# Batch 0 of a fused attention and FFN kernel: v scaled on GpSimd, numerators scaled and divided in PSUM, and all engines' work in a new order

## The chip, the core and the metric

One core of a Trainium2 chip. The time is that of one execution on the device, in microseconds (us), the median of several. The core's engines run at their own pace and wait for each other by semaphores: TensorE (PE, with its weight loads PEld), VectorE (DVE), ScalarE (ACT), GpSimd (POOL) and SyncE (SP, which here only issues DMAs). POOL and ACT issue DMAs too.

## The reference

Linear attention with a Hedgehog feature map, then a gated FFN. Batch 8, 8 heads, 576 positions, head size 64, 128 features; FFN 512 to 1536 to 512 over all 4608 tokens.

```python
def phi(x):
    proj = np.einsum('bhsd,df->bhsf', x, w_phi)
    proj = proj - np.max(np.abs(proj), axis=-1, keepdims=True)
    return np.concatenate([np.exp(proj), np.exp(-proj)], axis=-1)
q_p, k_p = (phi(q), phi(k))
kv = np.einsum('bhsf,bhsd->bhfd', k_p, v)
z = np.sum(k_p, axis=2)
num = np.einsum('bhsf,bhfd->bhsd', q_p, kv)
den = np.einsum('bhsf,bhf->bhs', q_p, z)[..., None] + 1e-06
attn = num / den                      # then heads side by side: x, 4608 x 512
out = (np.maximum(x @ w_gate, 0.0) * (x @ w_val)) @ w_out
```

## The kernel before

The order of all work is a table, ORDER, of some 2340 words; a loop reads it from left to right and calls for each word the function do_xx, which records one step. So the table fixes the order on every engine, DMA issues included; there is no other scheduler. `ke.0.1.2.0:0@kp0` means step ke with arguments batch 0, head group 1, token quarter 2, sign 0, in PSUM bank 0, with its output in buffer 0 of the ring kp. There are 8 PSUM banks, named by hand.

A batch goes through these steps (the first argument is the batch):

- Loads: lk, lm (k), lq, ln (q), wl (wv and wg in thirds of 512 columns) and wo on POOL's queue, with v of batch 0 (lv.0); lv and lw of the other batches on SP's.
- phi of k: the transposed k (kT) times w_phi on PE (k3 in batch 0, kr later), exponentials with both signs on ACT (ke, L688, into kp), the largest absolute value on DVE (kx, L696, into mk), and its exponentials on ACT (kk, L705, into ek). The heads stand in three groups: 0 to 1, 2 to 4, 5 to 7.
- v times ek: vs on POOL (L745, and vo L757 for the column of ones), vq on POOL for the last 64 positions (L773, into vr). In batch 0 before, head group 0 and vr were scaled on DVE instead (vd L726, vz L678), from an ek that ACT had put into PSUM (kp L716).
- kv on PE (L794), from kp, vs and vr, copied to SBUF by ACT (kc) or DVE (kd), both L805.
- phi of q: qb or qc on PE, qe on ACT (L869, into qp), qx on DVE (L877, the maximum), then qy, qz, qu and qw (ACT, L910, into cq: the factor between the two signs).
- numerators, per chunk of 128 tokens: before, all batches had nu on PE (L917, both signs side by side, in three head groups), nt on DVE (L938: the second sign times cq, into t), nv on DVE (L948: first sign plus t, into u), nr on DVE (L956, reciprocal of the denominator) and nx on POOL (L960, division, into xu).
- xu is transposed: in batch 0 by PE (xp) and a copy (xa on ACT L1011, xc on DVE L1005), later by DMA (xt).
- FFN of batch 0: in quarters of tokens and groups of four 128-column blocks, pv and pg on PE (L1224: 16 matmuls each, with wv and wg), pa (ACT L1239), pb (DVE L1245: relu times val, into h), fo (L1256). Batches 1 to 8 (8 are the left-over tokens of all batches): fv and fg (L1097), va on ACT or vb on DVE (the copy of val), ga (DVE L1118). Batches 7 and 8 are multiplied by a scheme of seven products for eight (fi, L1194), and so is the second FFN product (fw, L1361), with sums made on POOL (ps, xs, wt).
- zz multiplies zeros on PE (L455), in otherwise idle time ahead of the first FFN product.

Of the kernel before, what the change touches and what calls it, by code (L numbers as in the profile page):

```python
# [17 lines left out]
wd kh.0:1@kT0 sl k3.1.0:45 ke.0.1.0.0:4@kp0 w1:6 kg.1:2 kx.0.1.1:5@mk0 kx.0.1.0:4 wa:6 zz.2:7  # L18
k3.1.1:01 ke.0.1.3.0:1 lm.0.1 kx.0.1.2:0 zz.3:3 k0.2:2 lq.0.1 ke.0.1.3.1:1 k1.2:2@kT1 ke.0.1.0.1:4
zz.3:7 k0.0:6 ke.0.1.2.1:0 ke.0.1.1.1:5 k3.2.1:37 ke.0.1.2.0:0 kx.0.1.3:1 ms.2 lw.0.0 lw.0.1  # L20
k1.0:6@kT2 zz.5:4 k3.0.1:21 kk.0.1.0@ek0 k3.0.0:04 ke.0.1.1.0:5 ke.0.0.3.0:1@kp1 q0.1:5 lq.0.0
kx.0.2.3:7@mk1 kx.0.2.2:3 kk.0.1.1 ke.0.2.2.0:3@kp2 kx.0.0.0:0@mk2 kx.0.0.2:2 lv.0.1 ke.0.2.2.1:3
ke.0.0.1.1:4 kx.0.0.3:1 q1.1:5@qT0 ke.0.0.1.0:4 ke.0.0.3.1:1 lv.0.0 zz.6:6 q0.0:6 kx.0.0.1:4 wl.0.1
zz.4:3 k3.2.0:31 lv.0.2 ke.0.2.3.0:7 ke.0.0.2.1:2 ke.0.0.0.1:0 q1.0:6@qT1 ke.0.2.3.1:7 kx.0.2.1:1
zz.1:5 qb.1.1:5 zz.3:4 qb.0.1:4 kx.0.2.0:3 ke.0.0.0.0:0 zz.2:7 qb.0.0:0 qx.0.0.1:4 ke.0.0.2.0:2
zz.1:6 qb.1.0:2 qx.0.1.1:5 zz.7:7 qy.0.1:6 kp.0.0.0:0 ke.0.2.0.0:3 lk.1.3 kk.0.2.1@ek1 kp.0.0.1:0
kk.0.2.0 ke.0.2.1.1:1 vo.1@vs0 qx.0.1.0:2 qe.0.0.1.0:4@qp0 ke.0.2.0.1:3 qe.0.0.1.1:4 lq.1.2
qe.0.1.0.0:2@qp1 qe.0.1.0.1:2 vs.0.1.0 qz.0.1:6@my0 zz.4:7 qb.0.3:7 qx.0.0.0:0 zz.2:6 qy.0.0:3
vd.0.0.0:0@vs1 qz.0.0:3@my1 vs.0.1.1 qe.0.1.1.1:5 vp.0:0 qu.0.1@mz0 ke.0.2.1.0:1 qe.0.1.1.0:5 wl.0.0
vz.0:0 qb.0.2:6 zz.2:4 qb.1.3:3 zz.2:4 qb.1.2:2 vd.0.0.1:0 qu.0.0@mz1 vz.1:0 qe.0.1.3.0:3@qp2  # L30
vo.2@vs2 qw.0.0@cq0 qx.0.0.3:7 qx.0.0.2:6 qe.0.0.0.0:0 vs.0.2.1 zz.7:4 kv.0.0:1 qx.0.1.3:3 lw.1.1
vs.0.2.0 kc.0.0:1@kv0 kt.1.1@kT3 qe.0.0.0.1:0 kv.0.2:5 kv.0.1:4 qe.0.0.2.1:6@qp3 lm.1.1 kc.0.2:5
wl.1.1 kc.0.1:4 nu.0.0.0:1 nt.0.0.0:1@t0 zz.1:0 nu.0.0.2:5 qw.0.1 qx.0.1.2:2 qe.0.0.2.0:6
qe.0.1.3.1:3 nu.0.0.1:0 nv.0.0.0:1@u0 zz.2:4 nu.0.1.2:4 lv.1.2 nu.0.1.0:6 qe.0.1.2.1:2 nt.0.0.1:0@t1
lm.1.0 nt.0.0.2:5@t2 qy.0.2:1 nv.0.0.1:0 qe.0.0.3.0:7 nv.0.0.2:5 nt.0.1.0:6@t3 zz.2:3 nu.0.1.1:3
qy.0.3:0 nr.0.0@r0 qe.0.1.2.0:2 qz.0.2:1@my2 nv.0.1.0:6@u1 qz.0.3:0@my0 qu.0.2@mz2 zz.5:5
kr.1.1:1265 qe.0.0.3.1:7 nt.0.1.2:4@t0 nt.0.1.1:3@t1 qw.0.2 wl.1.0 nu.0.2.2:0 nx.0.0@xu0 nv.0.1.2:4
xp.0.0:7 nv.0.1.1:3 nt.0.2.2:0@t2 ke.1.1.3.1:5@kp3 nr.0.1@r1 nu.0.2.1:4 xa.0.0:7 nt.0.2.1:4@t3
nu.0.2.0:3 ke.1.1.0.1:1 nt.0.2.0:3@t0 qu.0.3@mz1 ke.1.1.0.0:1 pv.1.0:7 nv.0.2.1:4@u2 nv.0.2.2:0
nv.0.2.0:3 nu.0.3.1:4 qw.0.3 ke.1.1.1.0:2 nx.0.1@xu1 kx.1.1.0:1@mk3 xp.0.1:0 pa.1.0:7@val0  # L40
kx.1.1.3:5 pv.0.0:3 nr.0.2@r2 xa.0.1:0 nt.0.3.1:4@t1 nu.0.3.0:1 kx.1.1.1:2 nt.0.3.0:1@t3
ke.1.1.3.0:5 nu.0.3.2:7 kx.1.1.2:6 pa.0.0:3@val1 nt.0.3.2:7@t2 pv.1.1:0 nx.0.2@xu2 lw.1.0
nv.0.3.0:1@u0 xp.0.2:5 ke.1.1.1.1:2 pv.0.1:3 nv.0.3.2:7 pa.1.1:0@val2 pg.1.0:2 qt.1.1@qT2 ku.1@kT2
kk.1.1.0@ek2 ke.1.1.2.1:6 nv.0.3.1:4 pa.0.1:3@val3 lm.2.0 kt.1.0 nr.0.3@r0 nx.0.3@xu3 kk.1.1.1
qc.1.1:1073 ke.1.1.2.0:6 wl.0.2 pg.1.1:4 xa.0.2:5 pv.0.2:6 vo.1.1@vs3 qx.1.1.0:1 wl.1.2 pb.1.0:2
qe.1.1.1.0:0@qp4 qe.1.1.3.1:3@qp1 qe.1.1.0.0:1@qp0 qe.1.1.1.1:0 qx.1.1.2:7 pa.0.2:6@val0 xp.0.3:5
pb.1.1:4 qx.1.1.1:0 qe.1.1.0.1:1 ln.0.1 qe.1.1.3.0:3 pv.1.2:2 xc.0.3:5 pg.0.0:4 lm.2.1 kr.1.0:6105
lv.1.3 pa.1.2:2@val2 kt.1.2@kT1 qe.1.1.2.0:7@qp3 ke.1.0.3.1:5@kp2 ln.0.0 pb.0.0:4 qe.1.1.2.1:7
ke.1.0.0.0:6 pv.0.3:2 kx.1.0.1:1@mk4 qx.1.1.3:3 ke.1.0.2.0:0 lv.1.0 ke.1.0.2.1:0 pg.0.2:4 kx.1.0.0:6
qt.1.0@qT1 kx.1.0.2:0 ke.1.0.3.0:5 pg.0.1:7 pb.0.1:7 pa.0.3:2@val1 pv.1.3:3 ke.1.0.1.0:1 pg.1.3:2  # L50
kx.1.0.3:5 ke.1.0.1.1:1 ke.1.0.0.1:6 qc.1.0:0167 pb.0.2:4 pg.1.2:5 pa.1.3:3@val3 fv.0.9:3 pg.0.3:4
pb.1.3:2 kk.1.0.0@ek3 qx.1.0.0:0 kk.1.0.1 pb.1.2:5 qx.1.0.1:1 qe.1.0.3.0:7 lk.2.3 lv.1.1 vs.1.1.1
qe.1.0.3.1:7 qe.1.0.2.1:6 vs.1.1.0 qx.1.0.3:7 qe.1.0.0.0:0 qe.1.0.0.1:0 fv.0.10:2 va.0.9:3@val0 wo.0
# [233 lines left out]
def kernel(  # L287
# [700 lines left out]
    def xT_cols(b, i):  # L988
        return xT(b)[:, :, P * i : P * (i + 1)]
# [488 lines left out]
```

## Time and profile before

| | |
|---|---|
| runs | 360.67, 360.89 and 361.22 us; median 360.89 |
| the profiled execution's own time | 360.87 us |
| its span, first to last instruction | 359.1 us |
| granted TensorE clock, mean | 0.999 |
| chain that ended last, by engine | PE 85%, DVE 8%, ACT 2%, DMA 2%, POOL 1% |
| moved over HBM | 37.81 MB read, 9.44 MB written |

The profile is of one execution. A matmul's end is modelled, so a row of several matmuls shows some 0.2 us more than the time from one to the next group. In a timeline the columns are start, duration from the first start to the last end, engine, line, operation, what it writes and reads, and how many; brackets hold idle time of the engine ahead of it and what ended it. Rows of groups have busy time and the mean in ns. Line numbers are of the kernel before; in the new kernel the lines behind the insertions are larger (the xT copy is L1050 there, and the steps that begin with b are new).

### The profile page before, as it was taken

The page shows a single profiled execution, that of the slowest core. Times are in us where ns is not written, and L with a number is a line of the kernel's source. Part 1 is how long each engine was busy: PE and PEld are TensorE (multiplying, and loading weights), DVE is VectorE, ACT ScalarE, POOL GpSimd, SP SyncE. Part 2 cuts the span into 40 slices and gives each one's busy share as a digit, 9 for nine tenths or more (in the row PEclk, how much of TensorE's full clock was granted, in tenths as well). Part 3 has the DMA queues.
Part 4 walks back from the last instruction along what each step waited for, and adds up shares of the span by engine and source line. Part 5 has one row for each costly group of instructions (what it writes and reads, how often), then busy time and mean ns, then how long its engine had stood idle before and what let it go on. Part 6 is the DMA issues. An engine that isn't in the chain of part 4 may idle for free.

```text
span 359.1 us, 10076 instructions
## 1 busy us (share of the span) xinstructions
PE 352.9 (98%) x3876; PEld 222.2 (62%) x3876; DVE 312.9 (87%) x721; ACT 235.8 (66%) x564; POOL 325.6 (91%) x393
## 2 busy tenths in 40 slices
PE   8999999999999999999999999999999999999996
PEld 6678966445575656765576546666656566444684
DVE  5999999989999999999997999999898853898744
ACT  3999996986698869786897269656861424454310
POOL 8674988999999999976999589989999999999994
PEclk9999999999999999999999999999999999999999
DMA  7999999990947494369215980778300221600017
GB/s 124 257 198 204 164 199 159 180 164 7 178 68 157 53 157 95 68 127 135 58 39 105 158 136 2 176 107 103 62 0 16 45 59 25 227 0 2 0 31 206
DMA packets 90770, 38.16 MB, mean 106 GB/s; under 512 B 64226, under 2 KB 86370, under 8 KB 90722
## 3 DMA queue, kind: packets, MB, share of 16 engines
q0 software_dynamic: 33504, 15.03, 32.5%
q1 hardware_dynamic: 56754, 21.83, 27.7%
q10 hardware_dynamic: 464, 0.66, 0.8%
q8 instruction: 30, 0.49, 0.6%
q14 instruction: 18, 0.15, 0.1%
HBM read 37.81 MB, written 9.44 MB: 132 GB/s over the span
## 4 chain that ended last, share of the span: by engine, by line
PE 85%; DVE 8%; ACT 2%; DMA 2%; issue 1%; POOL 1%; SPq 0%; DVEq 0%
PE bank L1097 35%; PE bank L1361 18%; PE bank L1194 10%; PE bank L794 5%; PE bank L1224 4%; PE bank L917 3%; PE bank L592 2%; PE bank L854 2%; PE bank L1256 2%; ACT kp L688 2%; DMA w64f<-in_w_phi_dram 2%; DVE t L938 1%; DVE u L948 1%; DVE h L1118 1%; DVE mk L696 1%
## 5 line engine op out<-in xcount | busy, mean ns | idle before, releaser
L688 ACT ACTIVATE kp<-bank 128x384 bf16<-128x384 f32 x192 | 84.2, 513 | 16.6 <-DVE mk L696 7.4
L1097 PE MATMUL bank<-xTs,wv 128*128 128x512 bf16 x304 | 75.7, 379 | 0.0
L1097 PE MATMUL bank<-xTs,wg 128*128 128x512 bf16 x304 | 74.6, 379 | 0.0
L869 ACT ACTIVATE qp<-bank 128x512 bf16<-128x512 f32 x128 | 69.9, 627 | 6.5 <-PE bank L854 4.2
L1118 DVE SCALAR_TENSOR_TENSOR h<-bank,val 128x512 bf16<-128x512 f32 x90 | 60.5, 680 | 6.7 <-PE bank L1097 4.5
L1112 ACT CAST val<-bank 128x512 bf16<-128x512 f32 x59 | 35.1, 594 | 33.4 <-PE bank L1097 30.4
L745 POOL TENSOR_TENSOR vs<-vn,ek 128x780 bf16<-128x780 f32 (+2 forms) x40 | 53.8, 1366 | 0.8 <-ACT ek L705 0.4
L696 DVE TENSOR_REDUCE mk<-bank 128x3 f32<-128x384 f32 x96 | 49.1, 542 | 0.2
L960 POOL TENSOR_TENSOR xu<-u,r 128x512 bf16<-128x512 f32 x36 | 37.4, 1045 | 11.6 <-DVE r L956 11.5
L1361 PEld LDWEIGHTS <-h 128*128 128x128 bf16 x432 | 41.1, 98 | 10.0 <-issue 2.6
L1097 PEld LDWEIGHTS <-wg 128*128 128x128 bf16 x304 | 27.8, 98 | 30.2 <-issue 1.3
L1097 PEld LDWEIGHTS <-wv 128*128 128x128 bf16 x304 | 27.6, 98 | 27.3 <-issue 0.9
L877 DVE TRANSPOSE_TENSOR_REDUCE maxq<-bank 128x16 f32<-128x512 f32 x56 | 36.9, 690 | 0.1
L948 DVE TENSOR_TENSOR u<-bank,t 128x195 f32<-128x195 f32 (+1 forms) x108 | 32.9, 327 | 1.8 <-POOL xu L960 0.9
L1361 PE MATMUL bank<-wo,h 128*128 128x256 bf16 x260 | 32.5, 273 | 0.0
L1337 POOL TENSOR_TENSOR vs<-h 128x256 bf16<-128x256 bf16 x42 | 28.0, 671 | 3.7 <-DVE h L1118 3.6
L938 DVE TENSOR_TENSOR t<-bank,cq 128x195 f32<-128x195 f32 (+1 forms) x96 | 29.6, 326 | 1.9 <-PE bank L917 1.2
L917 PEld LDWEIGHTS <-qp 128*128 128x128 bf16 x512 | 23.1, 98 | 10.2 <-issue 0.5
L1337 POOL TENSOR_TENSOR h<-h,vs 128x256 bf16<-128x256 bf16 x44 | 28.6, 676 | 0.0
L1337 POOL TENSOR_TENSOR vs<-vs,h 128x256 bf16<-128x256 bf16 x42 | 28.0, 672 | 0.6
L1337 POOL TENSOR_TENSOR h<-h 128x256 bf16<-128x256 bf16 x42 | 27.9, 674 | 0.3
L917 PE MATMUL bank<-kv,qp 128*128 128x65 bf16 x512 | 26.0, 193 | 0.2 <-ACT kv L805 0.2
(156 smaller groups left out, 686.0 us busy)
## 6 DMA issues: line engine op xcount, KB each, us to landing
vn<-in_v_dram SPq DMA_DIRECT2D x24, 256.0 KB, 4.3
out_dram<-xTs SPq DMA_DIRECT2D x17, 256.0 KB, 3.0
kn<-in_k_dram POOLq DMA_DIRECT2D x7, 512.0 KB, 8.1
qn<-in_q_dram POOLq DMA_DIRECT2D x7, 512.0 KB, 8.0
out_dram<-obp SPq DMA_DIRECT2D x14, 256.0 KB, 2.6
wv<-in_moe_w_val_dram POOLq DMA_DIRECT2D x3, 512.0 KB, 9.4
wg<-in_moe_w_gate_dram POOLq DMA_DIRECT2D x3, 512.0 KB, 8.8
wo<-in_moe_w_out_dram POOLq DMA_DIRECT2D x3, 512.0 KB, 8.3
```

The lines of the kernel that those rows point to most:

```text
L688: nc.scalar.activation(kp_of(3 * b + j)[:, i, s].rearrange("p n f -> p (n f)"), bank[bk[0]][:, 0 : 3 * F], AF.Exp, scale=(1.0, -1.0)[s],)
L696: nc.vector.tensor_reduce(mk_of(3 * b + j)[:, :, i], bank[bk[0]][:, 0 : 3 * F].rearrange("p (n f) -> p n f", f=F), axis=AX.X, op=ALU.max, ...
L745: nc.gpsimd.tensor_tensor(vs_of(3 * b + j)[:, s, 0:n].rearrange("p n i e -> p (n i) e")[:, :, 0:e], src[:, lo:hi].rearrange("p h i e -> p ...
L869: nc.scalar.activation(qp_of(4 * b + i)[:, s, 4 * hq : 4 * hq + 4].rearrange("p h m -> p (h m)"), bank[bk[0]], AF.Exp, scale=(1.0, -1.0)[s],)
L877: nc.vector.tensor_reduce((maxq0[:, i] if b == 0 else maxq)[:, :, i, 4 * hq : 4 * hq + 4].rearrange("p t h -> p h t"), bank[bk[0]].rearran ...
L917: nc.tensor.matmul(bank[bk[0]][:, E * n : E * (n + 1)], lhsT=qp_of(4 * b + i)[:, s, h, :], rhs=kv_of(b)[:, h, s, 0:E],)
L948: nc.vector.tensor_tensor(u_of(serial(b, i))[:, lo:hi], parts(bk, n)[:, :, 0], t_of(3 * serial(b, i) + g)[:, 0:n], op=ALU.add,)
L960: eng.tensor_tensor(xu_of(n).rearrange("p (h d) -> p h d", d=D), u_of(n)[:, :, 0:D], r_of(n).to_broadcast([P, H, D]), op=ALU.mult,)
L1097: nc.tensor.matmul(bank[bk[0]], lhsT=w[:, dc, P * f : P * f + P], rhs=xT(g)[:, dc, :], start=(dc == 0), stop=(dc == NDC - 1),)
L1118: nc.vector.scalar_tensor_tensor(h2_of(g, f), bank[bk[0]], 0.0, val_of(NFC * g + f), op0=ALU.max, op1=ALU.mult)
L1337: eng.tensor_tensor(sum_of(g, n, j), a, b, op=op)
L1361: nc.tensor.matmul(bank[bk[0]][:, col : col + HN], lhsT=x[:, P * u : P * (u + 1)], rhs=w, start=(n in (1, 5, 6) and u == us[0] and j == 0) ...
```

## The change

Three things, all in batch 0, and a new table.

1. All of v is scaled on POOL: the steps kp, vd, vp and vz go, kk, vo, vs and vq of head group 0 come. The kv copies of groups 0 and 1 go from ACT to DVE (kd), the last xT copy from DVE to ACT (xa).
2. The numerators of a chunk are made in two halves of four heads. bu.0.i.g.1 multiplies the second sign into a bank, bt scales it there by cq on DVE, bu.0.i.g.0 adds the first sign to it in the same bank, br takes the reciprocal and bx divides from the bank into xu, on DVE. The steps nu, nt, nv, nr and nx of batch 0 go.
3. The table is made anew from its first phi step to its end, with the DMA issues in the same order among themselves. In the later batches 11 copies of val go from DVE to ACT and 4 the other way; of the kv copies three go to DVE and one back.

```diff
-wd kh.0:1@kT0 sl k3.1.0:45 ke.0.1.0.0:4@kp0 w1:6 kg.1:2 kx.0.1.1:5@mk0 kx.0.1.0:4 wa:6 zz.2:7
+wd lm.0.1 ms.2 lq.0.1 lw.0.0 lw.0.1 lq.0.0 lv.0.1 lv.0.0 wl.0.1 lv.0.2 kg.1:2@kT0 kh.0:1 zz.1:4
+zz.7:5 k3.1.0:67 ke.0.1.0.1:6@kp0 k3.1.1:01 kx.0.1.1:7@mk0 kx.0.1.3:1 kx.0.1.0:6 zz.2:3 zz.2:4
...
+    HALVES = ((0, 4), (4, 8))
...
+    def do_bu(bk, b, i, g, s):
+        lo, hi = HALVES[g]
+        for h in range(lo, hi):
+            n = h - lo
+            nc.tensor.matmul(
+                bank[bk[0]][:, E * n : E * (n + 1)],
+                lhsT=qp_of(4 * b + i)[:, s, h, :],
+                rhs=kv_of(b)[:, h, s, 0:E],
+                start=(s == 1 and h == lo),
+                stop=(h == hi - 1),
+                skip_group_check=(s == 0),
+            )
+    def part(bk, g):
+        lo, hi = HALVES[g]
+        return bank[bk[0]][:, 0 : E * (hi - lo)].rearrange("p (h e) -> p h e", e=E)
+    def do_bt(bk, b, i, g):
+        lo, hi = HALVES[g]
+        nc.vector.tensor_tensor(
+            part(bk, g),
+            part(bk, g),
+            scales(b, i)[:, lo:hi][:, :, None].to_broadcast([P, hi - lo, E]),
+            op=ALU.mult,
+        )
+    def do_br(bk, b, i, g):
+        lo, hi = HALVES[g]
+        nc.vector.reciprocal(r_of(serial(b, i))[:, lo:hi], part(bk, g)[:, :, D : D + 1])
+    def do_bx(bk, b, i, g):
+        n, (lo, hi) = serial(b, i), HALVES[g]
+        nc.vector.tensor_tensor(
+            xu_of(n).rearrange("p (h d) -> p h d", d=D)[:, lo:hi],
+            part(bk, g)[:, :, 0:D],
+            r_of(n)[:, lo:hi].to_broadcast([P, hi - lo, D]),
+            op=ALU.mult,
+        )
```

Other functions that the diff adds (do_bm, do_fa and so on) are not called by the new table. With zz.6 ahead of that line, 14 products of zeros (6 + 1 + 7) stand on PE between the first transposition and k3.1.0, and 6 did before.

On ACT, at the end of batch 0's exponentials: qp are exponentials of q, kv the kv copies, kp_84 exponentials of k of batch 1, xTs the first copy of the transposed chunk. Before:

```order
L805 CAST kv_104<-bank_68 128x6x65
L805 CAST kv_104<-bank_67 128x6x65
L910 ACTIVATE cq_115<-mz_120 128x8
L869 ACTIVATE qp_113<-bank_69 128x512
L869 ACTIVATE qp_112<-bank_66 128x512
L869 ACTIVATE qp_113<-bank_65 128x512
L869 ACTIVATE qp_112<-bank_70 128x512
L869 ACTIVATE qp_113<-bank_65 128x512
L869 ACTIVATE qp_112<-bank_70 128x512
L910 ACTIVATE cq_115<-mz_122 128x8
L688 ACTIVATE kp_84<-bank_68 128x384
L1011 COPY xTs<-bank_70 128x4x128
```

And now:

```order
L869 ACTIVATE qp_113<-bank_66 128x512 x2
L805 CAST kv_104<-bank_64 128x6x65
L910 ACTIVATE cq_115<-mz_120 128x8
L688 ACTIVATE kp_84<-bank_68 128x384
L688 ACTIVATE kp_84<-bank_69 128x384
L910 ACTIVATE cq_115<-mz_121 128x8
L688 ACTIVATE kp_84<-bank_67 128x384
L688 ACTIVATE kp_84<-bank_69 128x384
L688 ACTIVATE kp_84<-bank_70 128x384
L688 ACTIVATE kp_84<-bank_67 128x384
L1050 COPY xTs<-bank_69 128x4x128
```

The last kv copy has moved behind all exponentials of q, and six exponentials of batch 1 stand ahead of the first xT copy where one stood.

On POOL, from the q load of batch 1 to the two gate loads (vs and vr are scaled v, wv and wg the FFN weights, km and kn parts of k). Before:

```order
L496 DMA qn_73<-in_q_dram 128x8x256
L745 TENSOR_TENSOR vs_97<-vn_75,ek_91 128x12x64 x2
L558 DMA wv<-in_moe_w_val_dram 128x4x512
L757 CAST vs_99<-ek_92 128x24
L745 TENSOR_TENSOR vs_99<-vn_75,ek_92 128x12x64 x2
L508 DMA km_72<-in_k_dram 128x1x128
L558 DMA wg<-in_moe_w_gate_dram 128x4x512
L508 DMA km_72<-in_k_dram 128x1x128
L558 DMA wg<-in_moe_w_gate_dram 128x4x512
```

And now, to the first of the gate loads:

```order
L558 DMA wv<-in_moe_w_val_dram 128x4x512
L745 TENSOR_TENSOR vs_97<-vn_75,ek_91 128x12x64 x2
L757 CAST vs_98<-ek_92 128x2x8
L745 TENSOR_TENSOR vs_98<-vn_75,ek_92 128x8x64
L773 TENSOR_TENSOR vr_103<-vm_76,ek_92 64x8x65
L745 TENSOR_TENSOR vs_98<-vn_75,ek_92 128x8x64
L773 TENSOR_TENSOR vr_103<-vm_76,ek_92 64x8x65
L745 TENSOR_TENSOR vs_99<-vn_75,ek_93 128x12x64
L757 CAST vs_99<-ek_93 128x24
L745 TENSOR_TENSOR vs_99<-vn_75,ek_93 128x12x64
L508 DMA km_72<-in_k_dram 128x1x128
L558 DMA wg<-in_moe_w_gate_dram 128x4x512
```

Five operations of head group 0 have come in ahead of the gate loads, and the wv load has gone ahead of the first scaling.

More of the change, by code (lines that the diff above doesn't have):

```diff
@@ L1077, in do_mn, with do_bm @@
                     )
+    def do_bm(bk, p, g, s):
+        lo, hi = HALVES[g]
+        for h in range(lo, hi):
+            n = h - lo
+            for bb in range(2):
+                nc.tensor.matmul(
+                    bank[bk[0]][SM * bb : SM * (bb + 1), E * n : E * (n + 1)],
+                    lhsT=qr_of(p)[:, s, h, 2 * bb : 2 * bb + 2, :].rearrange("p i t -> p (i t)"),
+                    rhs=kv_of(2 * p + bb)[:, h, s, 0:E],
+                    start=(s == 1 and h == lo),
+                    stop=(h == hi - 1),
+                    skip_group_check=(s == 0),
+                )
     h2_at = {f: f for f in range(NFC)}
@@ L1120, in do_ga @@
         )
+    SEEDED = ()
     PAIRS = ((8, 7),)
```

557 lines of the change are left out of this document (291 added, 266 removed).

## The prediction

> **What bounds the kernel now.** I read the busy shares first, then the stretches of 9 us, then each engine's timeline over the first 40 us.
>
> ```profile
> PE 352.9 (98%) x3876; PEld 222.2 (62%) x3876; DVE 312.9 (87%) x721; ACT 235.8 (66%) x564; POOL 325.6 (91%) x393
> ...
> 9.00:18.00 9.00, 8.79 (x88) 5.48 (x85) 8.80 (x20) 8.92 (x29) 6.28 (x8) 1.00 1.24 256
> 18.00:27.00 9.00, 8.72 (x157) 6.38 (x160) 8.91 (x26) 8.97 (x21) 6.37 (x7) 1.00 1.34 199
> 27.00:36.00 9.00, 8.80 (x179) 7.89 (x168) 8.98 (x30) 8.59 (x23) 4.28 (x5) 1.00 1.14 203
> 45.00:54.00 9.00, 9.00 (x133) 5.46 (x131) 9.00 (x19) 8.90 (x24) 8.03 (x10) 1.00 1.34 201
> ...
> 99.00:108.00 9.00, 8.94 (x118) 7.04 (x117) 8.94 (x24) 8.73 (x25) 8.92 (x12) 1.00 0.46 68
> 108.00:117.00 9.00, 8.83 (x101) 5.11 (x94) 8.94 (x16) 7.60 (x17) 8.83 (x9) 1.00 0.78 161
> ...
> 288.00:297.00 9.00, 8.58 (x93) 6.20 (x92) 4.43 (x13) 1.87 (x4) 8.32 (x12) 1.00 0.22 57
> ```
>
> The columns after the stretch are its length, then busy time (instructions) of PE, PEld, DVE, ACT, POOL. From 45 us on PE is full. Its missing time stands in a few rows: 0.06, 0.17 and 0.42 us in those shown, some 0.8 us over all the rest of the span. PE's work is the same before and after (the sixteen 65-column products of a chunk are regrouped, not fewer). So the end can move in two ways only: by when PE begins to be full, and by what later waits are lost or added.
>
> Before 28 us PE looks busy, but much of that is filler: multiplications of zeros. PE's timeline shows where real work takes over.
>
> ```profile
> 1.06 3.38 PE L455 MATMUL bank<-zero 128*128 128x256 bf16 x15 [1.06 <-DVE zero L441]
> ...
> 5.51 1.49 PE L455 MATMUL bank<-zero 128*128 128x256 bf16 x6
> 7.10 0.34 PE L668 MATMUL bank<-w,kT 64*128 64x128 bf16 x6
> ...
> 7.46 0.39 PE L455 MATMUL bank<-zero 128*128 128x256 bf16 x2
> ...
> 28.67 1.05 PE L1224 MATMUL bank<-xTs,wv 128*128 128x128 bf16 x16 [0.20 <-ACT xTs L1011]
> ```
>
> 28.67 us is the first FFN product (step pv); from there PE has work without a pause. It was released by ACT's copy of the transposed chunk (step xa). ACT and DVE have no gap from 9 to 27 us (8.92, 8.97; 8.80, 8.91 of 9.00): in this stage the order of work on ACT and DVE sets the time, not PE.
>
> **The change, part by part.** The normalization first. Twelve scalings, twelve additions, four reciprocals and DVE's scaling of v go; eight scalings in PSUM, eight reciprocals and eight divisions come.
>
> ```profile
> L938 DVE TENSOR_TENSOR t<-bank,cq 128x195 f32<-128x195 f32 (+1 forms) x12 | 3.6, 318 | 0.0
> L948 DVE TENSOR_TENSOR u<-bank,t 128x195 f32<-128x195 f32 (+1 forms) x12 | 3.4, 321 | 0.0
> L678 DVE TENSOR_TENSOR vr<-vm,bank 64x520 bf16<-64x520 f32 x2 | 1.4, 677 | 0.0
> L726 DVE TENSOR_TENSOR vs<-vn,bank 128x512 bf16<-128x512 f32 x2 | 1.3, 661 | 0.0
> ...
> L1216 DVE TENSOR_TENSOR val<-bank,u 128x512 bf16<-128x512 f32 x24 | 15.8, 684 | 4.6 <-PE bank L1194 3.4 <-ACT u L1210 1.2
> ```
>
> Removed from DVE: 3.6 + 3.4 + 1.4 + 1.3 = 9.7 us. Added: no row shows a DVE scaling from PSUM to PSUM. Between 318 ns for about 180 columns and 684 ns for 512, one of 260 columns lies near 0.40 us; the two ends are those rows themselves, 0.32 and 0.68. Sixteen (eight scalings, eight divisions) at 0.40 are 6.4 us, with 5.1 to 10.9 as ends. Two kv copies come over from ACT and the extra reciprocals cost about 0.1 each. DVE thus gains about 2 us at 0.40 and loses about 3 at the upper end. I take 0.40, the interpolation. This gain is worth only what DVE holds up, and in the new order it isn't DVE that ACT waits for, as follows.
>
> **The start of phi.** Eight more zero products stand ahead of the first phi(k) products (14 instead of 6). Fifteen took 3.38 us, one per 0.21; at 7.46 us two take 0.39, one per 0.11. So the array doubled its rate between 6.8 and 7.46 us. Six end at 6.8; eight more end at 7.7 (0.11 each) to 8.5 (0.21 each). Before, 7.10 was set by w64 and cost no filler. I take 7.72: ACT's first exponential is 0.62 us later; bounds 0 and 1.4.
>
> The Trainium skill, "TensorE: Matmul & The Clock Gate", Part 1, says that the array starts at half rate and that the window after which it is released is free-running, so that the point differs from run to run by about half a microsecond. The trace agrees on the two rates (0.21 and 0.11 us). By that rule the same 14 zeros would end near 7.1 in a run released at 5.5 us, and this term would be nothing there; no run here shows the spread.
>
> **ACT up to the first FFN product.** ACT's timeline and its groups from 7.46 to 27.2 us:
>
> ```profile
> 7.46 0.49 ACT L688 ACTIVATE kp<-bank 128x384 bf16<-128x384 f32 x1 [1.86 <-PE bank L668]
> ...
> 8.20 2.40 ACT L688 ACTIVATE kp<-bank 128x384 bf16<-128x384 f32 x6
> ...
> 21.86 0.38 ACT L805 CAST kv<-bank 128x260 bf16<-128x260 f32 x1
> 22.12 1.13 ACT L869 ACTIVATE qp<-bank 128x512 bf16<-128x512 f32 x2
> 23.15 1.01 ACT L805 CAST kv<-bank 128x390 bf16<-128x390 f32 x2
> 24.05 0.21 ACT L910 ACTIVATE cq<-mz 128x8 f32<-128x8 f32 x1
> ...
> 27.11 0.21 ACT L910 ACTIVATE cq<-mz 128x8 f32<-128x8 f32 x1
> ...
> 28.03 0.59 ACT L1011 COPY xTs<-bank 128x512 bf16<-128x512 bf16 x1 [0.16 <-PE bank L997]
> ...
> L688 ACT ACTIVATE kp<-bank 128x384 bf16<-128x384 f32 x24 | 10.1, 542 | 1.9 <-PE bank L668 1.9
> L869 ACT ACTIVATE qp<-bank 128x512 bf16<-128x512 f32 x16 | 8.6, 621 | 0.0
> L805 ACT CAST kv<-bank 128x390 bf16<-128x390 f32 (+1 forms) x3 | 1.4, 453 | 0.0
> ```
>
> From 7.46 to 27.11 ACT did 24 exponentials of k, 16 of q, three kv copies and small ones: 19.65 us. Before, the first kv copies came at 21.86 and 23.15, with five exponentials of q behind them, so that the numerators ran beside those. After, the one kv copy left to ACT (kc.0.2, heads 5 to 7, which every chunk's second half needs) stands behind all 24 and all 16. Two kv copies go, one per 0.26 and 0.45 us (21.86 to 22.12; half of 23.15 to 24.05): 19.65 - 0.71 = 18.94. From 8.08 that gives its end at 27.0.
>
> Then ACT has two more cq and six exponentials of batch 1 ahead of the first xT copy. Six take 6 x 0.384 = 2.3 us ((2.40 - 0.48) / 5 apart), the cq 0.2: the copy starts at 29.5, and PE's first FFN product 0.64 later (28.03 to 28.67), at 30.15 against 28.67: **+1.5 us**. DVE is ready before that: scaling, second half, reciprocal, division and transposition behind 27.0 end near 29.2. With the six behind the copy the copy would start at 29.2, for +1.2; that and a gate opened early (0.9) are this term's lower ends, 2.3 with the zeros at half rate its upper one.
>
> POOL is not the bound either, but near it:
>
> ```profile
> 13.14 0.88 POOL L496 DMA_DIRECT2D qn<-in_q_dram  x1 [1.23 <-PE bank L822]
> 14.03 2.92 POOL L745 TENSOR_TENSOR vs<-vn,ek 128x768 bf16<-128x768 f32 x2
> ...
> 18.13 2.91 POOL L745 TENSOR_TENSOR vs<-vn,ek 128x768 bf16<-128x768 f32 x2
> ...
> 21.73 0.79 POOL L558 DMA_DIRECT2D wg<-in_moe_w_gate_dram  x1
> ...
> 23.22 0.78 POOL L558 DMA_DIRECT2D wg<-in_moe_w_gate_dram  x1
> ...
> L773 POOL TENSOR_TENSOR vr<-vm,ek 64x520 bf16<-64x520 f32 x14 | 14.8, 1059 | 1.7 <-ACT ek L705 0.7 <-POOL h L1337 0.5
> ...
> L745 POOL TENSOR_TENSOR vs<-xTs,ek 128x512 bf16<-128x512 f32 x2 | 2.1, 1044 | 0.0
> ```
>
> Its first scaling starts again near 14.1 (the q load goes out 0.8 us earlier, one wv load of 0.8 is now ahead). Then four scalings of 768 columns at 1.45, two of 512 at 1.04, two of vr at 1.06 and two casts, 0.4 together, make 10.4 us: the last vs ends at 24.5 instead of 21.0, and the kv product behind it on PE about a microsecond later, still one before ACT comes to its copy.
>
> Behind those scalings (0.7 and 2.2 us behind, as before) the two gate loads go out at 25.2 and 26.7 instead of 21.73 and 23.22.
>
> ```profile
> 30.13 0.89 PE bank L1224 x16
> ...
> DMA to landing us min/median/max: 6.2/9.1/11.3
> ```
>
> The first row is one such product in the chain of waits (16 matmuls), the second the landing of the wv and wg loads. At 9.1 us the gate weights are there at 34.3 and 35.8. PE comes to them after four wv products (3.6 us) and some small work (1.3 us) at 35.0, and to the second third one product and one transposition later, at 36.1. The landing is hidden at the median; at 11.3 the second costs 1.9. I take +0.2, a tenth of that.
>
> **Later.** Two zero products now stand in batch 1's numerators, where PE is full: 2 x 0.11 = +0.2. The re-made order can save at most the 0.8 us of shown waits and a few short ones that modelled ends hide; in batch 0's wake DVE has 2 us of slack where PE waited at 99 to 117 us (0.23), and ahead of the three-product stage (288 to 297: 0.42) the new order puts four PE steps between the last gate product and the sum that POOL makes of it, where one stood. I take -0.6. The last steps (two half products, an addition, an output DMA) are as before: 0.
>
> Sum: 1.5 + 0.2 + 0.2 - 0.6 = +1.3 us. The profiled execution took 360.87 us (span 359.1 and 1.8 around it), 0.02 under the median of the runs. 360.87 + 1.3 = **362.2 us**.
>
> **The rivals.** *Faster.* The relief of DVE reaches on: seven copies of val net go from DVE to ACT, and 2 us are saved at the start. For it: DVE is at 8.9 of 9.00 from 9 to 117 us. Against it: PE is full there. PE's later waits, the 0.8 us shown and the short ones that modelled ends hide (a dozen of 0.15 would be 1.8), all go: -2.6 instead of -0.6 gives 360.2. It decides when more than 2 us of them fall to DVE. Chance 0.18.
>
> *No change.* The zeros cost nothing in the timed runs and the later waits give the 0.8 us shown: 1.5 - 0.6 + 0.2 - 0.8 = +0.3, 361.2. Chance 0.24.
>
> *The gate weights are late.* PE stops at the gate products for 1.5 us more: 363.7. For it: the DMA column (1.14 to 1.34) shows full engines until 36 us, and the v loads of batch 1 now go ahead. Chance 0.12.
>
> The forecast has 0.46. Within 0.2% (0.72 us) a measurement of this kernel can't tell a change. Range: from the faster rival at 360.1 to the late weights at 363.8.
>
> **What would show it.** The first phi exponential on ACT near 8.1 us and not 7.5; the kv copy on ACT ending near 27; the first product from xTs and wv near 30.1; gate products without a gap before them; PE at 8.9 or more of 9.00 in 288 to 297. Wrong if the first FFN product starts by 29 us, or if ACT waits before 27 us for PE or DVE (then it is slower yet).

## The result: 374.6 us, slower by 3.8%, and the profile after

| | before | after |
|---|---|---|
| median | 360.78 us (4 runs, 360.01 to 361.22) | 374.62 us (4 runs, 373.83 to 375.07) |
| ratio to before, 95% interval | | 1.0384 [1.0356, 1.0412] |
| profiled execution, its span | 360.87, 359.1 us | 375.07, 373.3 us |
| granted TensorE clock, mean | 0.999 | 0.982 |

The prediction was 362.2, with 363.8 as the upper end: 12.4 us too low. The page of the changed kernel, its busy times:

```profile
PE 352.5 (94%) x3830; PEld 224.8 (60%) x3876; DVE 313.0 (84%) x708; ACT 237.3 (64%) x568; POOL 325.8 (87%) x394
```

And its windows of 9 us at the three places told below, with one more (288 to 297) in which PE had a gap before (columns as before; behind POOL's come the granted clock, the DMA share and GB/s):

```profile
18.00:27.00 9.00, 5.49 (x59) 3.45 (x58) 8.94 (x14) 6.74 (x17) 8.84 (x10) 0.79 1.32 210
27.00:36.00 9.00, 7.84 (x160) 7.09 (x158) 7.59 (x25) 6.41 (x19) 0.86 (x2) 0.83 1.25 200
108.00:117.00 9.00, 6.99 (x69) 5.11 (x66) 8.55 (x19) 7.49 (x18) 8.82 (x11) 1.00 0.75 91
117.00:126.00 9.00, 7.18 (x51) 3.61 (x54) 4.57 (x9) 5.11 (x10) 6.83 (x9) 0.81 0.45 122
225.00:234.00 9.00, 5.38 (x63) 3.58 (x62) 4.43 (x8) 4.22 (x12) 8.99 (x10) 0.81 0.01 2
288.00:297.00 9.00, 8.91 (x56) 4.76 (x57) 6.68 (x16) 1.17 (x2) 8.92 (x13) 1.00 0.21 56
```

Two of these windows in the kernel before, which the prediction does not show:

```profile
117.00:126.00 9.00, 9.00 (x119) 5.84 (x117) 8.82 (x20) 7.29 (x22) 8.93 (x13) 1.00 0.47 55
225.00:234.00 9.00, 9.00 (x114) 5.95 (x111) 8.93 (x23) 6.09 (x13) 8.91 (x14) 1.00 0.84 187
```

PE's busy total is about that of before (352.9) in a span that is 14.2 us longer, so its work did not grow: PE waits. It does so at three places, and at each the granted clock falls below 1.00; in the kernel before every one of these windows had 1.00. How long PE ran at half clock can be worked out from the rows. Windows of 2 us that lie inside such a stretch (24 to 30, 119 to 121) have 0.50. From 117 to 126 us 0.19 of 9 us are missing, that is 1.71 us, so the clock was at 0.50 for 3.42 us. From 225 to 234 it is the same. From 18 to 36 (0.21 and 0.17) it is 6.84 us, twice as long.

PE's timeline has one wait of more than 2 us at each place (rows 1, 3 and 4); row 2 is the first FFN product:

```profile
25.11 0.39 PE L410 MATMUL bank<-w,sel 64*128 64x128 bf16 x2 [2.50 <-DVE sel L403]
34.17 1.05 PE L1278 MATMUL bank<-xTs,wv 128*128 128x128 bf16 x16
118.60 0.42 PE L1150 MATMUL bank<-xTs,wv 128*128 128x512 bf16 x1 [3.38 <-DMA xTs<-xu]
228.58 0.38 PE L794 MATMUL bank<-vs,kp 128*128 128x65 bf16 x4 [3.39 <-POOL vs L745]
```

**Place 1, the start.** The first FFN product comes at 34.17 us instead of 28.67. PE waits for sel, a small bf16 copy from SBUF to SBUF on DVE (step sl, used by w1). It used to stand at 6.86 us, where POOL only issued DMAs, and took 0.32 us (DVE's row of before):

```profile
6.86 0.32 DVE L403 COPY sel<-ident 64x256 bf16<-64x256 bf16 x1
```

The new table puts it among POOL's scalings. DVE's timeline, then POOL's:

```profile
21.53 3.52 DVE L403 COPY sel<-ident 64x256 bf16<-64x256 bf16 x1
...
20.85 1.05 POOL L773 TENSOR_TENSOR vr<-vm,ek 64x520 bf16<-64x520 f32 x1
21.86 1.47 POOL L745 TENSOR_TENSOR vs<-vn,ek 128x768 bf16<-128x768 f32 x1
23.28 0.28 POOL L757 CAST vs<-ek 128x24 bf16<-128x24 f32 x1
23.44 1.47 POOL L745 TENSOR_TENSOR vs<-vn,ek 128x768 bf16<-128x768 f32 x1
24.85 0.76 POOL L508 DMA_DIRECT2D km<-in_k_dram  x1
```

The copy ends at 25.05, within 0.2 us of POOL's last tensor operation (24.91). PE stands still; ACT then waits 1.66 us for w1's bank on PE, and 0.60 and 1.25 us for DVE; and the kv sums behind run at half clock.

**Place 2, batch 2's FFN.** PE waits for the last of four DMA transpositions (xt.2.2). SP issued it at 112.25, 0.4 us behind a 512 KB load of q that POOL issued at 111.85. The DMA view of the changed kernel at that point, with KB each and the us from issue to landing:

```profile
qn<-in_q_dram POOLq DMA_DIRECT2D x1, 512.0 KB, 7.1
xTs<-xu SPq DMA_TRANSPOSE x1, 6.3
```

Before, the same transposition (the view at 105.6 us):

```profile
xTs<-xu SPq DMA_TRANSPOSE x1, 2.4
```

The old table also has this q load as the word ahead of this transposition. But POOL, which was behind with other work, came to it only at 109.07 us, 3.5 us after SP had issued the transposition.

**Place 3, batch 6's kv.** PE waits for POOL's vs, and POOL for the load of v of batch 6. These four loads had been free to go since 200.2 us, when POOL finished with the old v. On SP's queue they stand behind transpositions of batch 5, which wait for their xu, and the issue of one of which took 4.85 us. POOL's row, and SP's:

```profile
225.01 3.52 POOL L745 TENSOR_TENSOR vs<-vn,ek 128x780 bf16<-128x780 f32 x3 [5.68 <-DMA vn<-in_v_dram]
...
212.53 0.57 SPq L531 DMA_DIRECT2D vn<-in_v_dram  x1
213.20 4.85 SPq L1031 DMA_TRANSPOSE xTs<-xu  x1
218.10 1.19 SPq L531 DMA_DIRECT2D vn<-in_v_dram  x2
```

The loads stood between the same transpositions before. There the last two were issued at 210.0 and 210.6, and POOL came to v of batch 6 only at 215.78, without a wait (POOL's row of before):

```profile
215.78 2.52 POOL L745 TENSOR_TENSOR vs<-vn,ek 128x520 bf16<-128x520 f32 x2
```

In the changed kernel POOL was ready for it at 219.33 (225.01 less the wait), 0.6 us after the last load was issued at 218.7.

### The profile page after: what moved, and what is told of

Read it like the earlier page. It is cut to its first block, busy times and chain, and to the rows that moved or that the text cites. A ratio compares the mean times of both kernels' runs of the same rounds, so it can differ in the third digit from the quotient of the medians.

```text
span 373.3 us, 10015 instructions
## 1 busy us (share of the span) xinstructions
PE 352.5 (94%) x3830; PEld 224.8 (60%) x3876; DVE 313.0 (84%) x708; ACT 237.3 (64%) x568; POOL 325.8 (87%) x394
## 4 chain that ended last, share of the span: by engine, by line
PE 76%; DVE 8%; POOL 4%; ACT 4%; DMA 3%; issue 3%; SPq 0%; POOLq 0%; DVEq 0%
PE bank L1150 29%; PE bank L1416 17%; PE bank L1248 10%; PE bank L794 5%; PE bank L1278 4%; ACT kp L688 3%; PE bank L917 2%; PE bank L854 2%; PE bank L592 2%; DMA xTs<-xu 2%; DMA vn<-in_v_dram 2%; DVE t L938 1%; PE bank L455 1%; DVE u L948 1%; DVE mk L696 1%
## 5 line engine op out<-in xcount | busy, mean ns | idle before, releaser
L745 POOL TENSOR_TENSOR vs<-vn,ek 128x780 bf16<-128x780 f32 (+3 forms) x42 | 56.2, 1350 | 11.6 <-DMA vn<-in_v_dram 5.7
L1165 ACT CAST val<-bank 128x512 bf16<-128x512 f32 x66 | 39.1, 604 | 39.2 <-PE bank L1150 25.6
L960 POOL TENSOR_TENSOR xu<-u,r 128x512 bf16<-128x512 f32 x32 | 33.3, 1044 | 9.3 <-DVE r L956 6.5
L948 DVE TENSOR_TENSOR u<-bank,t 128x195 f32<-128x195 f32 (+1 forms) x96 | 29.7, 327 | 1.2
L794 PEld LDWEIGHTS <-kp 128*128 128x128 bf16 x640 | 23.8, 102 | 8.2 <-issue 4.7
L794 PE MATMUL bank<-vs,kp 128*128 128x65 bf16 x512 | 24.5, 199 | 3.4 <-POOL vs L745 3.4
L938 DVE TENSOR_TENSOR t<-bank,cq 128x195 f32<-128x195 f32 (+1 forms) x84 | 25.7, 325 | 1.3 <-ACT cq L910 0.6
```

What stands on the lines that cost most here:

```text
L745: nc.gpsimd.tensor_tensor(vs_of(3 * b + j)[:, s, 0:n].rearrange("p n i e -> p (n i) e")[:, :, 0:e], src[:, lo:hi].rearrange("p h i e -> p ...
L794: nc.tensor.matmul(out_ps[:, h - lo, s, :], lhsT=lhsT, rhs=rhs, start=(at == 0), stop=(at == 2 * n * (C + 1) - 1),)
L1165: nc.scalar.copy(val_of(NFC * g + f), bank[bk[0]])
```

## The experiments: a few words at a time

**The three places, mended singly and together.** All are the changed kernel with words of the table moved.

```diff
 e1   wd +sl ...  qx.0.0.3:1 -sl
 e2   -lq.4.2 xt.2.2 ... vq.3.1 +lq.4.2
 e3   vs.5.2.0 +lv.6.0 +lv.6.3 +lv.6.1 +lv.6.2 ...  -lv.6.0 ... xt.5.1 -lv.6.3 xt.5.3 -lv.6.1 -lv.6.2 xt.5.2
 e4   e1, e2 and e3 together
```

> The changed kernel with one word moved: the copy sel<-ident on VectorE goes back to its old place, right behind the cast w64<-w64f, at about 6.9 us, where POOL only issues DMAs. Theory 1 (the copy is held while POOL runs tensor operations): it takes about 0.3 us instead of 3.52; w1 on PE no longer waits 2.50; the first product xTs x wv of the FFN moves from 34.17 to 30.3-31.0, and, with the half-rate matmuls behind the wait gone too, the time falls by 3 to 4 us, to 370.6-371.6. Theory 2 (the start is late because of the new order on ACT and POOL, and the copy only fills a wait that is there anyway): the copy is short here too, but the product does not come before 33.5 and the time falls by less than 0.7 us. The waits at 114.8 and 224.8 stay under both.

> The changed kernel with one word moved: the load of q of batch 4 (qn, on POOL's queue, issued 0.4 us ahead of the last DMA transposition of batch 2) goes behind the two vr products on POOL, some 2.3 us later. Theory 1 (that load fills the DMA engines ahead of the transposition): the transposition issued near 112.25 lands within 2.5 us instead of 6.3, PE's wait of 3.38 for xTs at 118.60 goes below 0.5, the 8 half-rate matmuls behind it go back to full rate, and the time falls by 4 to 5.5 us, to 369.1-370.6. Theory 2 (the transposition is late by itself or through SP): it still lands near 118.5 and the time stays within 0.7 us of the changed kernel.

> The changed kernel with four words moved: the four loads of v of batch 6 go on SP right behind the last product that reads the old v (POOL, near 200 us), ahead of the transpositions of batch 5, as they stood in part in the kernel before. Theory 1 (they were issued at 208.8, 212.5, 218.1 and 218.7 because they stood behind transpositions on SP's queue, in a stretch where the DMA engines are full): issued at 200-203, all landed before 215; POOL's wait of 5.68 and PE's of 3.39 at 228.58 go, and the time falls by 3.5 to 5 us, to 369.6-371.1. Theory 2 (the DMA engines are full from 204 to 225 whatever the order, so only the order of landing changes): another operand (transposed x of batch 5, or k or q) comes late instead and less than 1.5 us is won.

> The three moves together. If the three places are the whole loss and are independent, the falls add up: 10.5 to 14.5 us, to 360.1-364.1, with 362 the likeliest (the blind forecast: 362.2); the granted clock is 1.00 at all three places. If moving one wait only uncovers the next (rival), it stays above 365.

| | median us | ratio to before [95%] | to after |
|---|---|---|---|
| e1, copy early | 372.04 (369.79 to 373.44) | 1.0305 [1.0263, 1.0346] | -2.6 |
| e2, q load late | 369.66 (369.54 to 370.33) | 1.0248 [1.0229, 1.0267] | -5.0 |
| e3, v loads early | 369.70 (368.97 to 371.46) | 1.0253 [1.0219, 1.0286] | -4.9 |
| e4, all three | 362.40 (361.68 to 363.37) | 1.0052 [1.0028, 1.0076] | -12.2 |

The single gains add up to 12.5, the three together give 12.2 of the 13.8 us lost: three separate causes, and most of the loss, as far as e1's spread (369.79 to 373.44) lets one add. At places 2 and 3 the parts come out too: the wait and the missing clock are 3.38 + 1.71 and 3.39 + 1.71, 5.1 us each, where 5.0 and 4.9 were won.

In e1 the copy took 0.33 us again and the first FFN product came at 29.07, earlier than expected. Yet the median fell by 2.6 us where 3 to 4 were expected, and the trace does not show why: it is of e1's fastest execution, 4.8 us below the changed kernel, though PE waited 1.26 us for the gate weights in it. In e2 the transposition landed in 2.4 us and the FFN of batch 2 began without a wait; in e3 POOL's products with v of batch 6 did.

PE in e1, at the gate weights:

```profile
36.46 1.96 PE L1278 MATMUL bank<-xTs,wg 128*128 128x128 bf16 x32 [1.26 <-DMA wg<-in_moe_w_gate_dram]
```

PE in e2, the FFN of batch 2:

```profile
114.72 3.63 PE L1150 MATMUL bank<-xTs,wv 128*128 128x512 bf16 x16
```

POOL in e3, v of batch 6:

```profile
217.85 3.53 POOL L745 TENSOR_TENSOR vs<-vn,ek 128x780 bf16<-128x780 f32 x3
```

e3's trace has a surprise: its start is the changed kernel's, but here the copy was not held. DVE reached it at 21.23, while POOL was going from one product to the next (rows of DVE and POOL):

```profile
21.23 0.24 DVE L403 COPY sel<-ident 64x256 bf16<-64x256 bf16 x1
...
20.27 1.04 POOL L745 TENSOR_TENSOR vs<-vn,ek 128x512 bf16<-128x512 f32 x1
21.27 1.13 POOL L773 TENSOR_TENSOR vr<-vm,ek 64x520 bf16<-64x520 f32 x1
```

It got in, and POOL's vr took 1.13 instead of 1.05 us. In the changed kernel the copy came 0.3 us later, in the middle of vr, and was passed over at all three changes of instruction that followed; so it was in e2 (3.61 us) and in e5 below (3.62).

In this execution some of the gain is place 1's, at most the 1.7 us by which the second FFN step began earlier (61.13 against 62.82). By the clock it was an exception. A stretch of 3.4 us at half clock costs 0.005 of the mean clock. The changed kernel, with four such lengths, has 0.982; e3 has 0.994 in this execution and 0.985 in its three others, as if there only place 3's were gone. These three hold the two values (369.15 and 370.25) between which the median lies, so the 4.9 us are most likely place 3's alone. Only one of the four has a trace.

**Is it POOL that holds the copy?** The kernel before, with copies into sel added that nobody reads:

```diff
 q1.0:6@qT1 +sl ...  vd.0.0.0:0@vs1 +sf ...  qu.0.0@mz1 +sl ...  qx.0.0.2:6 +sl
+    def do_sf(bk):     # as do_sl, from the float32 identity
```

> The kernel before with four copies into sel added on VectorE, which nobody reads any more at that point: bf16 from ident behind the second qT copy (DVE near 14.4, while POOL runs its products from 14.03 to 16.95); float32 from identf behind the first scaling of v on DVE and bf16 from ident behind the second vz or mz step (DVE near 18.9 and 20, while POOL runs its products from 18.13 to 21.04); bf16 from ident behind the next-to-next kx or qx step, near 22 or later, where POOL issues DMAs alone. Theory 1 (a VectorE copy from SBUF to SBUF is held while POOL's tensor operations follow one another): the first takes some 2.5 us, the second and the third end only with POOL's run or in a gap between two of its operations, the last takes 0.32 us; the neighbours on DVE that read PSUM keep their old lengths. Theory 2 (the 3.52 us came from something else in the changed kernel, its bank or a DMA that reads ident): all four take 0.24 to 0.35 us.

DVE's four copies with its scaling of v, and POOL's runs (rows of both):

```profile
13.76 2.78 DVE L403 COPY sel<-ident 64x256 bf16<-64x256 bf16 x1
20.02 0.64 DVE L726 TENSOR_TENSOR vs<-vn,bank 128x512 bf16<-128x512 f32 x1
20.59 0.99 DVE L1440 CAST sel<-identf 64x256 bf16<-64x256 f32 x1
23.21 0.24 DVE L403 COPY sel<-ident 64x256 bf16<-64x256 bf16 x1
25.56 0.29 DVE L403 COPY sel<-ident 64x256 bf16<-64x256 bf16 x1
...
13.46 2.92 POOL L745 TENSOR_TENSOR vs<-vn,ek 128x768 bf16<-128x768 f32 x2
16.32 0.81 POOL L558 DMA_DIRECT2D wv<-in_moe_w_val_dram  x1
...
18.53 2.90 POOL L745 TENSOR_TENSOR vs<-vn,ek 128x768 bf16<-128x768 f32 x2
21.38 0.75 POOL L508 DMA_DIRECT2D km<-in_k_dram  x1
```

Both copies that began in a run of POOL ended 0.1 to 0.2 us after it; the third, while POOL issued DMAs, and the fourth, while POOL was idle, took 0.24 and 0.29. (The third slid out of POOL's run and so tells the same as the fourth.) The float32 cast was held as well. DVE's scaling of v (L726), which reads SBUF and PSUM, took its usual 0.64 inside the second run. The hold is shown, and in a kernel without the change. It ran once, in 365.19 us, with the clock at 0.50 from 20 to 26 us. The Trainium skill, "SBUF — State Buffer", section "Who interferes with whom", says that copies and casts on VectorE may enter a two-port mode and then share a port pair with GpSimd, which the first to start keeps for its whole instruction. The trace agrees on who is held; by that rule the copy of the changed kernel would have started at 21.90, when vr ended, but it waited through three more instructions of POOL.

**Is q's load enough by itself?** The reverse, on the kernel before: its q load goes, in the table, ahead of the last two transpositions.

```diff
 nx.2.2@xu3 +lq.4.2 ...  -lq.4.2 xt.2.2
```

> The reverse of the move of the q load, on the kernel before: its load of q of batch 4 goes from 109.07 to just behind the last nx of batch 2 (near 103.9), ahead of the last two transpositions of batch 2 on SP, and nothing else is changed. Theory 1 (a load of 512 KB issued ahead of a transposition delays its landing by some 4 us): the last transposition lands at 110-113 instead of 108.1, the first FFN product of batch 2 starts at 111-114 instead of 109.91 with a wait of 1.5 to 3.5 us for xTs, and the time rises by 1.5 to 5 us. Theory 2 (it is not the load): the transpositions land as before and the time stays within 0.5 us of the kernel before.

362.69 us (362.42 to 363.23), ratio 1.0060 [1.0045, 1.0075]: +2.1. The last transposition took 6.9 us to land (104.71 to 111.59) instead of 2.4, and PE waited where it had not. (The one before it, whose issue began at 102.65, 0.6 us ahead of the load's, took 8.6.)

```profile
111.63 1.90 PE L1097 MATMUL bank<-xTs,wv 128*128 128x512 bf16 x7 [1.61 <-DMA xTs<-xu]
```

The load alone is enough. Before, the transposition landed at 108.1, 1.8 us ahead of PE's product at 109.91, so that much of the delay stayed hidden. The clock stayed at 1.00 behind the wait of 1.61.

**What a wait costs beyond itself.** The changed kernel with 28 products of zeros ahead of that FFN.

```diff
+zz.28:3 fv.2.2:3
```

> The changed kernel with 28 multiplications of zeros (3.0 us at 0.107 us each) put on PE in front of the first FFN product of batch 2, where PE waits 3.38 us for the last transposition. They do no work of the reference. Theory 1 (PE's own clock falls after it has been idle and costs extra behind the wait): the granted clock in 117-126 goes from 0.81 to 1.00, the 512-column matmuls behind the wait take half as long, the first fv product still starts near 118.6, and the time falls by 1.2 to 2.0 us. Theory 2 (the matmuls behind the wait are slow for want of operands, not of clock): no change, within 0.4 us.

PE's row, and then the window of 9 us:

```profile
119.40 3.61 PE L1150 MATMUL bank<-xTs,wv 128*128 128x512 bf16 x15 [0.38 <-DMA xTs<-xu]
```

```profile
117.00:126.00 9.00, 8.51 (x92) 5.22 (x95) 5.71 (x12) 5.18 (x11) 7.44 (x9) 1.00 0.60 140
```

From the first fv to the kv sums behind it (L794) this took 4.31 us (119.40 to 123.71), and 6.01 in the changed kernel (118.60 to 124.61). So the clock costs 1.7 us behind a wait of 3.38: theory 1 in the trace. The first fv itself came 0.8 us later than in the changed kernel, so that the kv sums came only 0.9 us earlier. The price is not fixed: in e1 a wait of 3.34 us at the same place was followed by 6.8 us at half clock, and from the first fv to the kv sums it took 7.26 us (114.88 to 122.14), 2.9 more than in e2 (4.33, with no wait).

The whole time does not show it: 374.54 (371.47 to 376.17), ratio 1.0376 [1.0332, 1.0421], too wide to tell 1.7 us. The mean clocks of the four executions go from 0.980 to 0.991, so they did not run equally long at half clock.

**The remaining 1.7 us of e4.** Three kernels with e4 as the base, to see what holds its start.

```diff
 e6   vq.0.0 +wl.1.1 kv.0.0:2 ... vs.0.2.1 +wl.1.0 ... lm.1.1 -wl.1.1 ... lm.1.0 -wl.1.0
 e7   e6, and -zz.1:4 -zz.7:5
 e8   e4, and -zz.1:4 -zz.7:5
 e9   e8, and bx.0.0.1:3 +gx +lv.1.2 ...    # gx: a 128-byte transfer on SP that reads xu of chunk 0
```

> All three moves, and the two loads of gate weights earlier on POOL: the first ahead of the last two products with v (issued near 21.5 instead of 25.18), the second ahead of the two loads of k of the memory tokens (near 25.2 instead of 26.68). Theory 1 (the landing of the gate weights at 36.97 is the next limit behind the three places): PE's wait of 0.56 ahead of the gate products goes and the time falls by 0.4 to 1.0 us below all three moves, to 361.4-362.0. Theory 2 (the DMA engines are full at that time, or the later products with v make PE wait for POOL): no gain beyond 0.2 us, or 0.5 us lost at kv of the last heads.

> As the kernel with the gate weights early, and without the eight multiplications of zeros on PE ahead of the first phi product of k (8 x 0.107 = 0.86 us on PE). Theory 1 (they delay the first exponential by 0.45 us and all of the start stage with it): the first ke on ACT at 7.4 instead of 7.9 and the time 0.3 to 0.6 us lower than with the gate weights early alone, 360.8-361.7. Theory 2 (the second operand, k of the memory tokens, lands at 8.3 anyway and PE or DVE waits for it): no change, within 0.2 us.

> All three moves, and without the eight multiplications of zeros ahead of the first phi product of k. Theory 1 (they set the first exponential): the first ke on ACT goes from 7.9 (or 7.3 to 8.1, by when k lands) to 0.4-0.5 us earlier for the same landing of k, and the time falls by 0.3 to 0.6 us, to 361.8-362.1. Theory 2 (k of the memory tokens, landing at 8.3, sets the start): within 0.2 us of all three moves, 362.4.

> All three moves, without the eight multiplications of zeros, and with the loads of v of batch 1 and 2 on SP (issued from 20.0 on, backed up behind each other until 30.5) held back by a 128-byte transfer that reads the first finished x of batch 0, so that they are issued near 28.5. Theory 1 (the gate weights land late because these loads fill the DMA engines from 20 on): the gate loads, still issued near 25.2 and 26.7, land before 31 and 34 instead of 31.8 and 36.97, the wait of 0.56 goes, v of batch 1 still lands before 40.8 where POOL first reads it, and the time falls by another 0.4 to 1.2 us below the kernel without the zeros, to 360.4-361.6, level with the kernel before. Theory 2 (v of batch 1 comes late then, or x sets the gate products): POOL waits near 41 for v, or nothing is won, and the time is 361.8 or more.

| | median us | ratio to before [95%] |
|---|---|---|
| e6 | 363.33 (362.39 to 364.26) | 1.0073 [1.0049, 1.0097] |
| e7 | 362.72 (361.95 to 363.61) | 1.0061 [1.0038, 1.0083] |
| e8 | 362.66 (361.41 to 364.15) | 1.0061 [1.0037, 1.0085] |

None is faster than e4. In e6 the gate weights came early, but k of the memory tokens was now behind them: DVE waited for it, with batch 0's divisions queued behind, and PE's first gate product waited longer than in any other run (rows of DVE and PE of e6):

```profile
37.09 0.31 DVE L581 STREAM_TRANSPOSE kT<-km 128x128 f32<-128x128 f32 x1 [2.48 <-DMA km<-in_k_dram]
37.76 1.05 PE L1278 MATMUL bank<-xTs,wg 128*128 128x128 bf16 x16 [2.26 <-DVE xu L1020]
```

In e8 the zeros are gone and the first product comes at 29.59 (30.33 in e4, but 29.07 in e1, both with the zeros); PE only reaches the gate weights sooner:

```profile
37.34 1.96 PE L1278 MATMUL bank<-xTs,wg 128*128 128x128 bf16 x32 [1.63 <-DMA wg<-in_moe_w_gate_dram]
```

So in e1, e4 and e8 PE's longest wait left at the start is for the landing of the gate weights, while the DMA engines are full (the share is 1.22 to 1.35 from 9 to 36 us in e4). Taking this wait away did not win the 1.7 us. In e6 the wait for DVE took its place. e9's six executions lie at 362.14 and 362.48 us and, four of them, between 367.95 and 371.32, so its median cannot be compared; in the profile of the one of 362.14 the gate wait is gone, but the clock was at 0.50 from 22 to 24 us and the first product came at 30.47 (29.59 in e8). What parts e9's executions, and what holds the last 1.7 us, stays open. No version beat the kernel before.

**One part alone.** The kernel before with v scaled on POOL, in the old order:

```diff
-kp.0.0.0:0 -kp.0.0.1:0 -vd.0.0.0:0@vs1 -vd.0.0.1:0 -vp.0:0 -vz.0:0 -vz.1:0
+kk.0.0.0@ek2 +kk.0.0.1 +vs.0.0.0@vs1 +vs.0.0.1 +vo.0 +vq.0.0 +vq.0.1    # each in the place of its like
```

> One part of the change alone, in the old order: on the kernel before, the v of the first two heads, its ones columns and the v of the memory tokens are scaled on POOL in the places where VectorE did it (two products of 1.04 us, two of 1.05 and a cast of 0.16 more on POOL, some 3.3 us less on VectorE); numerators and the order of all else are as before. Theory 1 (POOL sets the start: what VectorE saves there is not on the path): POOL's last product with v ends near 25.3 instead of 21.04, PE waits 2.5 to 4 us for it ahead of the kv sums, the gate loads are issued 4.3 us later, the clock may fall behind the wait, and the time rises by 3 to 5 us, to 363.6-365.6. Against the three moves together (362.4) this says what the new order is worth at the start. Theory 2 (VectorE sets the start): PE's wait is below 1 us, the first FFN product comes before 28.7 and the time is 360.7 or less.

366.68 us (364.52 to 367.38), ratio 1.0161 [1.0121, 1.0200]: +6.2, more than expected. PE waited for POOL, and the kv sums behind that ran at half clock (24 to 30 us at 0.50):

```profile
25.57 0.38 PE L794 MATMUL bank<-vs,kp 128*128 128x65 bf16 x4 [2.78 <-POOL vs L745]
```

The first FFN product came at 34.08, as late as in the changed kernel. The wait and the clock together come to it, a sum that no run takes apart: 6.8 us at half clock are 3.4 us lost, and 2.78 + 3.4 are 6.2. Theory 1 holds: what DVE saves there was not on the path.

## Why the prediction was wrong, step by step

- **The failed step, "ACT up to the first FFN product".** It added up ACT's work as if ACT never waited, and took every moved instruction at its old duration. The moved copy sel went unpriced: it cost 3.52 us instead of 0.32 and held w1 on PE and with it ACT. The kv copy ended at 30.98 instead of 27.0, the first product came at 34.17 instead of 30.15. That is the event which the prediction named as its refutation (ACT waits before 27 us for PE or DVE). With the copy early the rest of the step holds: in e1 ACT took 18.8 us from its first exponential to the end of the kv copy (7.17 to 25.99), where 18.94 stood. That e4's product came at 30.33 is in part luck: its first exponential came at 7.33, 0.75 earlier than forecast, and ACT then waited 1.00 us for DVE ahead of 25.65.
- **The failed step, "Later".** It weighed only which of the old waits would go (-0.6), with no term for new ones. Two came, worth 5.0 (e2) and 4.9 us (e3): of the 14.2 us by which the span grew, 5.4 stand at the second FFN step's first product (57.46 to 62.82), and 8.8 come behind it, where this step had -0.4 in all. The words concerned stood in the same order in the old table: a 512 KB load right ahead of the last transposition, loads of v behind transpositions on SP. New were the times between them: the load now went out 0.4 us ahead of the transposition instead of 3.5 behind it, and POOL wanted v 0.6 us after the last load's issue instead of 5.2. That the DMA issues kept their order among themselves says nothing about such spare time. The old waits did go: 288 to 297 rose from 8.58 to 8.91, in e4 to 9.00.
- **The clock.** It was taken as full from 7 us on. Each wait of 2.5 us or more brought back half rate, for 3.4 or 6.8 us, which cost 1.7 us at place 2.
- **Gate weights.** Hidden in the changed kernel, since PE came so late (39.0, landing 33.75 and 37.56). With the copy mended PE waited 1.26, 0.56 and 1.63 us for them (e1, e4, e8) where +0.2 stood: in those kernels, not in the changed one, the rival with 0.12 was right on the mechanism.
- **The zeros.** The first exponential came at 7.91, 0.45 us later, where +0.62 stood. But kernels with all 14 zeros had it between 7.11 and 8.12 and those without the eight at 6.71 to 7.24, and e8 gained no time, since PE came to the gate weights sooner and waited for them.
- **Right.** A scaling of 260 columns in PSUM took 0.41 to 0.43 us (0.40), POOL's last vs ended at 24.91 (24.5), the gate loads went out at 25.60 and 27.09 (25.2 and 26.7).
- **The sum without the three accidents.** e4 is 362.40, the forecast 362.2: in its trace the start costs +2.25 us (first product of the second FFN step, 57.46 to 59.71), the later waits give back 0.75 (the span grew by 1.5). That the sum comes out, in part by luck, does not save the forecast: its range had no case for a new wait beyond the gate weights.
- **Slips that change nothing.** Six exponentials of q stood behind the kv copies of 23.15, not five; DVE's loss at the upper end is 9.7 - 10.9 - 0.9 - 0.4 = -2.5 us, not 3; the faster rival's own sum is 360.2, where the range says 360.1.

## What to carry to other kernels

When an order is made anew, go through each moved word with three questions: which engine runs beside it at its new place (a VectorE copy within SBUF beside GpSimd products took up to eleven times as long), which large load is now issued shortly ahead of a transfer that PE needs in two microseconds, and which waiting transfer on an in-order queue now stands ahead of a load that could go. The table's order does not answer the last two, for two engines' queues run at their own pace: compare the times. Behind a PE wait of some 3 us this kernel lost 1.7 to 3.4 us more to the clock. A forecast of a re-made order needs a term for waits that do not exist yet.

## What the runs showed of the hardware

- A VectorE copy or cast within SBUF that came while GpSimd ran tensor operations one after another waited through several of them (3.52, 3.61 and 3.62 us past three changes of instruction, 2.78 past one); once, at the moment of a change, it got in (0.24 us, e3). So the same program can take either way in two executions, by e3's clocks.
- A DMA transposition issued 0.4 us behind a 512 KB load landed with it, not after its own 2.4 us: 118.55 beside 118.92 us here, 111.59 beside 111.19 in the reverse run (1.4 us behind the load there).
- Behind PE's wait of 3.38 us its sixteen 512-column matmuls took 5.15 us (118.60 to 123.75), against 3.47 in e2 (114.72 to 118.19); with the wait filled by zeros the clock stayed at 1.00. In every trace here in which the clock fell between 9 and 350 us, the half rate lasted 3.4 or 6.8 us, worked out from the missing clock as above.
- The length of the wait alone does not decide. The clock stayed at 1.00 behind 1.61 us (the reverse run), 2.26 (e6, the gate products) and 2.27 (e1, place 3); it fell behind 2.10 (c1, ahead of 18.75 us), 2.23 (e5, place 3), 2.50, 2.78 and all those of 3.3 and more. The Trainium skill, "TensorE: Matmul & The Clock Gate", Part 1, says that the clock falls to half after an idle window of about 3.4 us that runs freely. The lengths of 3.4 and 6.8 us fit a window of that length, and one that runs freely would let nearly equal waits go either way; but shorter waits than 3.4 sufficed, with PE only partly busy around them (0.60 and 0.66 of 2 us in 22 to 26). In e4 the clock was at 0.54 from 22 to 24 us with no wait above 0.6; that stays open.
